# Loading and splitting the first pair of attention heads once for both heads

## Chip, cores and metric

One core of a Trainium2 chip runs the whole program. The metric is the device time of one execution in microseconds (us), lower is better. Three executions of the kernel before took 829.32, 829.61 and 830.26 us; the median is 829.61.

## The reference

Batch 2, 8 heads, sequence 1152, head size 64. Queries are averaged in pairs along the sequence, so each head has 576 query rows and 1152 keys. The attention output, laid out as 1152 tokens of 512 features, goes through a leaky-ReLU layer pair (512 to 2048 to 512) and then through four experts (512 to 1024 to 512), weighted by normalised probabilities.

```python
q_pool = q.reshape(B, H, S // 2, 2, D).mean(axis=3)
scores = (1 / sqrt(D)) * q_pool @ k.T
attn = softmax(scores)                    # row maximum taken off, 1e-9 in the denominator
x = (attn @ v)                            # to 1152 tokens x 512
x = leaky_relu(x @ w_in) @ w_out
out = sum_e p[:, e] * (relu(x @ w1[e]) @ w2[e])
```

All operands are float32. The kernel writes each operand of a product as a high part (cast to the multiplier's short float form) plus a low part (the rest), and adds up products of the parts.

## The kernel before

The eight (batch, pair of heads) units are called pairs, n = 0 to 7. A pair has nine tiles of 128 query rows: tiles 0 to 3 belong to the first head, tile 4 is half of each, tiles 5 to 8 belong to the second. Tile number i counts through all pairs, 72 in all. In this document S(i), T(i) and so on mean a step of tile i:

- S(i), `emit_s`: the score products on PE, in three chunks of 384 keys (L375). Then DVE copies the scores out of PSUM and takes their extreme, here called reduce(i) (L378).
- exp(i), `emit_exp`: the exponential on ACT (L384).
- sum(i) and norm(i), `emit_sum` and `emit_norm`: two tiny DVE steps (L388, L392) and then the scaling of the 128x1152 tile on POOL (L393).
- T(i), `emit_t`: nine transposes on PE (L414), three at a time; ACT casts each group to its high part (L418, `th`), and DVE takes the low part (L101, `tl`).
- AV, `queue_av` and `run_av`: the products of transposed scores with the values (L441), taken from a list a few at a time. When a chunk of the list is through, ACT and DVE add its two halves (L449, L450) and POOL splits the result (`xh`, `xl`).

The order on each engine's queue is the order in which the program issues instructions; it is written out by hand (`manual_schedule`), and an engine takes its queue strictly in that order. In the main loop, iteration i issues S(i+2) (in the first six tiles), sums and norms up to tile i+1, the steps in `early[i]`, T(i), some AV, exp(i+2) and then the steps in `steps[i]`.

For pairs 1 to 7 the keys and queries arrive once as 128 rows, 64 of each head (`rk_b`, `rq_b`), are split by `prep_pair` (POOL adds the two queries of each average, `q_add`, L306; ACT makes high parts; POOL makes low parts), and eight on-chip DMAs lay them out so that one product of 128 rows adds two terms: K of a head holds its high part in rows 0 to 63 and its low part in rows 64 to 127, and Q holds the same 64 rows twice. Two products per chunk then give all four terms. Tile 4 uses a block-diagonal operand `qmid` for its low terms.

Pair 0 is different. `first_pair` loads an input for each head that already holds the 64 rows twice (`q0`, `k0`, made on the host), so no on-chip copy is needed: `rk_b` and `rq_b` for head 0, `rk1` and `rq1` for head 1. SP issues these loads, then `load_v(0)`; ACT issues two pieces of keys. While they fly PE runs 18 transposes of no use (`keep_warm`). Head 0 is split in pieces, head 1 later in pieces between the first tiles (`k_hi(1, ..)`, `q_add(POOL, 1, ..)`, `q_hi(1, ..)`, `q_lo(POOL, 1, ..)` on L507 to L518 and in `steps`, `k_lo(DVE, 1, ..)` on L516 and L569). Because head 0 frees `rk_b` and `rq_b` early, `load_qk(1)` (L519), the keys and queries of pair 1, can start while head 1 is still being split.

The split of pair 1 begins in iteration 1: its `q_add` is in `early[1]`, on POOL's queue behind norm(2) and ahead of norm(3); its `k_hi` is in `steps[1]`.

Of the kernel before, what the change touches and what calls it, by code (L numbers as in the profile page):

```python
# [11 lines left out]
F32 = mybir.dt.float32  # L12
# [8 lines left out]
SQ = S // 2  # L21
# [12 lines left out]
def f32(ap):  # L34
    return ap.bitcast(F32)


@with_exitstack
def tile_kernel(ctx: ExitStack, tc: tile.TileContext, q, k, v, q0, k0, w_in, w_out, probs, w1, w2, out):
    nc = tc.nc  # L40
    PE, ACT, DVE, POOL, SP = nc.tensor, nc.scalar, nc.vector, nc.gpsimd, nc.sync

# [20 lines left out]
    rk1, rq1 = (at(f"r{i}1", 31872 + 2 * 2880 + 1152 * i, [S], F32) for i in range(2))  # L63
# [132 lines left out]
    with ExitStack() as actx:  # L196
# [17 lines left out]
        def two_heads(n, name):  # L214
            return [kv[name, h, n % 2] for h in range(2)]

        def load_qk(n):
            if n >= len(pairs):
                load_a()
                load_a()  # L220
                return
            b, p = pairs[n]
            rk, rq = rk_b, rq_b.rearrange("p (a b) -> p a b", a=2)
            SP.dma_start(rk, k[b, p])
            SP.dma_start(rq, q[b, p])
            raw[n] = (rk, rq)
# [8 lines left out]
        def first_pair():  # L235

            b, p = pairs[0]
            ks = kst[0] = two_heads(0, "k")
            rk = [rk_b, rk1]
            down = slice(64, 128)  # L240

            def halves(h, a, z):

                if h:
                    return rq1[:, a:z], rq1[:, SQ + a:SQ + z]
                o = next(x for x in (256, 128, 0) if a >= x)
                w = SQ - 256 if o == 256 else 128
                return rq_b[:, o + a:o + z], rq_b[:, o + w + a:o + w + z]
# [12 lines left out]
            load_v(0)

            def q_add(e, h, a, z):
                x, y = halves(h, a, z)
                e.tensor_tensor(x, x, y, op=ALU.add)

            def q_hi(h, a, z):
                hi(ACT, qst[0][:, 0, h, h * 64 + a:h * 64 + z], halves(h, a, z)[0])

            def q_lo(e, h, a, z):  # L270
                cs = slice(h * 64 + a, h * 64 + z)
                lo(e, qst[0][:, 1, h, cs], halves(h, a, z)[0], qst[0][:, 0, h, cs])

            def k_hi(h, a, z):
                hi(ACT, ks[h][:, a:z], rk[h][:, a:z])

            def k_lo(e, h, a, z):
                lo(e, ks[h][down, a:z], rk[h][down, a:z], ks[h][down, a:z])
            return q_add, q_hi, q_lo, k_hi, k_lo

        def prep_pair(n):


            rk, rq = raw.get(n, (None, None))

            rows = [slice(h * 64, h * 64 + 64) for h in range(2)]

            def k_hi():
                kh = k_hi_of[n] = kh_b[n % 2]
                hi(ACT, kh, rk)  # L290

# [12 lines left out]

            def q_add():
                POOL.tensor_tensor(rq[:, 0], rq[:, 0], rq[:, 1], op=ALU.add)  # L306

            def q_hi():
                hi(ACT, rq[:, 1].bitcast(F32R), rq[:, 0])

            def q_lo():
                lo(POOL, rq[:, 0].bitcast(F32R), rq[:, 0], rq[:, 1])
                t = qst[n % 2]
                for h in range(2):
                    r = slice(h * 64, h * 64 + 64)
                    hi(POOL, qmid[n % 2][r, r], rq[r, 0, (SQ - 64) * (1 - h):][:, :64])
                    for d in (slice(0, 64), slice(64, 128)):
                        SP.dma_start(f32(t[d, :, h, h * 64:h * 64 + SQ]), rq[r])

            def v_hi(h):  # L320
                if h == 0:
                    vst[n] = [t.rearrange("p (a b) -> p a b", a=NKB) for t in two_heads(n, "v")]
                a = h * 64
                hi(ACT, vst[n][h][:, :, a:a + 64], raw_v[n][:, :, h, :])

            def v_lo(h):
                a, c = h * 64, 64 - h * 64
# [30 lines left out]
        def emit_s(i):  # L358
            n, t = tiles[i]
            ps = three_banks(int(i == 1))  # L360
            Q, K = qst[n % 2], kst[n]
            if t < 4:
                use = [(0, t * 128)]
            elif t == 4:
# [2 lines left out]
                use = [(1, 128 + (t - 5) * 128)]  # L367
            for c in range(3):
                cs = slice(c * CW, (c + 1) * CW)
                mms = [(Q[:, j, h, c0:c0 + 128], K[h][:, cs]) for h, c0 in use for j in (1, 0)]  # L370
                if len(use) > 1 and n:

                    mms = mms[::2] + [(qmid[n % 2], k_hi_of[n][:, cs])]
# [93 lines left out]
                av.pop(0)[1]()  # L467

        with tc.manual_schedule():
            q_add, q_hi, q_lo, k_hi, k_lo = first_pair()  # L470

            DVE.memset(warm, 0.0)
            ACT.activation(warm, warm, AF.Exp)
# [27 lines left out]
            q_add(POOL, 0, 256, SQ)  # L501
# [46 lines left out]
            begin_at = {9 * m - P0: [m] for m in range(3, len(pairs))} | {P1: [0, 1], P2: [2]}  # L548
# [397 lines left out]
```

## Time and profile before

| | |
|---|---|
| median of three runs | 829.61 us |
| the profiled execution | 830.79 us |
| its span (first to last instruction) | 829.0 us |
| PE busy | 817.9 us |
| DVE, ACT, POOL busy | 567.7, 433.3, 407.2 us |
| mean granted TensorE clock | 0.998 of full |

The profiled execution took 830.79 us, 1.79 us more than its span, and 1.18 us more than the median of the runs. Busy time of PE is the sum of its instructions with modelled ends; a change is worth what it takes from or adds to the stretches in which PE waits or runs at a lower clock.

### The profile page before, as it was taken

To read this page: it belongs to the slowest core of one execution; us is meant where nothing else is said; L and a number is where in the kernel's file an instruction comes from. 1 tells how busy PE (TensorE), PEld (TensorE's weight loads), DVE (VectorE), ACT (ScalarE), POOL (GpSimd) and SP (SyncE) were. 2 spreads that over 40 slices of the span, in tenths; PEclk is the share of its full clock that TensorE was granted. 3 is DMA by queue.
4 is the path that set the end of the run, shared out by engine and by line. 5 is a ranking of instruction groups with operands and counts; after the bars stand their busy time and mean duration, and the time that the engine had idled before them with its cause. 6 is when DMAs were issued, how large, how long until landed. Compare 5 with 4: busy or idle time off the path is not lost.

```text
span 829.0 us, 13581 instructions
## 1 busy us (share of the span) xinstructions
PE 817.9 (99%) x5079; PEld 773.4 (93%) x5079; DVE 567.7 (68%) x955; ACT 433.3 (52%) x765; POOL 407.2 (49%) x363
## 2 busy tenths in 40 slices
PE   7899999999999999999999999999999999999998
PEld 6899999999999999999999989989898989989897
DVE  6899999999989898686766753627354453626332
ACT  7899999999985664334223632415051332505030
POOL 6798888888760487665550333306051332404020
PEclk9999999999999999999999999999999999999999
DMA  6626563664303333212220211203020111201012
GB/s 229 187 77 186 153 158 107 167 172 111 107 27 97 101 108 102 86 67 77 85 69 1 77 51 39 64 1 102 1 76 27 51 51 32 71 0 53 0 41 100
DMA packets 25969, 68.65 MB, mean 83 GB/s; under 512 B 2992, under 2 KB 7984, under 8 KB 25904
## 3 DMA queue, kind: packets, MB, share of 16 engines
q1 hardware_dynamic: 25616, 67.40, 27.6%
q8 instruction: 40, 0.66, 0.3%
q10 hardware_dynamic: 288, 0.39, 0.1%
q14 instruction: 25, 0.20, 0.1%
HBM read 48.91 MB, written 2.36 MB: 62 GB/s over the span
## 4 chain that ended last, share of the span: by engine, by line
PE 90%; DVE 6%; issue 1%; POOL 1%; DMA 1%; SPq 0%; ACT 0%; DVEq 0%; POOLq 0%; ACTq 0%
PE ps L762 22%; PE ps L375 8%; PE ps L807 8%; PE ps L809 8%; PE ps L808 8%; PE ps L441 8%; PE ps L414 7%; PE ps L191 4%; PE ps L190 4%; PE ps L659 4%; PE ps L660 4%; PE ps L192 4%; PE ps L661 4%; DVE e L378 2%; DVE tl L101 2%
## 5 line engine op out<-in xcount | busy, mean ns | idle before, releaser
L101 POOL TENSOR_TENSOR bb<-w2r,bb 128x512 fp32r<-128x512 f32 x32 | 40.8, 1296 | 258.9 <-ACT bb L94 258.9
L816 DVE SCALAR_TENSOR_TENSOR oacc<-ps,pw,oacc 128x512 f32<-128x512 f32 (+1 forms) x64 | 47.5, 742 | 100.4 <-PE ps L809 100.4
L101 DVE TENSOR_TENSOR tl<-ps,th 128x384 fp32r<-128x384 f32 (+1 forms) x240 | 111.9, 505 | 3.6 <-ACT th L418 2.8
L807 PE MATMUL ps<-bb,gg 128*128 128x512 f32 (+1 forms) x292 | 112.9, 387 | 0.0
L809 PE MATMUL ps<-bb,gg 128*128 128x512 f32 (+1 forms) x292 | 112.9, 386 | 0.0
L808 PE MATMUL ps<-bb,gg 128*128 128x512 f32 (+1 forms) x292 | 112.8, 386 | 0.0
L762 PE MATMUL ps<-yT,ws 128*128 128x288 f32 x768 | 111.5, 296 | 0.0
L762 PEld LDWEIGHTS ps<-yT,ws 128*128 128x128 f32 x768 | 105.7, 189 | 0.9 <-ACT cb L779 0.3
L393 POOL TENSOR_SCALAR e<-e,st 128x1152 f32<-128x1152 f32 x72 | 89.2, 1239 | 33.0 <-DVE st L392 18.3
L378 DVE TENSOR_SCALAR_CACHE_REDUCE e<-ps 128x1152 f32<-128x1152 f32 x72 | 97.4, 1354 | 9.0 <-PE ps L375 7.8
L418 ACT CAST th<-ps 128x384 fp32r<-128x384 f32 (+1 forms) x240 | 91.3, 459 | 13.6 <-PE ps L414 11.7
L768 ACT COPY ca<-ps 128x576 f32<-128x576 f32 x16 | 10.2, 639 | 167.1 <-PE ps L762 155.3
L375 PE MATMUL ps<-k,qst 128*128 128x384 f32 x438 | 94.4, 345 | 3.2 <-DVE e L378 1.6
L384 ACT ACTIVATE e<-e,st 128x1152 f32<-128x1152 f32 x72 | 91.3, 1268 | 2.5 <-DVE e L378 0.8
L414 PE MATMUL ps<-ident,e 128*128 128x128 f32 x648 | 83.8, 275 | 2.9 <-POOL e L393 2.2
L762 PE MATMUL ps<-yB,ws 128*128 128x288 f32 x576 | 84.4, 296 | 0.0
L375 PEld LDWEIGHTS ps<-k,qst 128*128 128x128 f32 x438 | 75.5, 190 | 8.1 <-DVE e L378 4.4
L414 PEld LDWEIGHTS ps<-ident,e 128*128 128x128 f32 x648 | 75.1, 141 | 7.5 <-POOL e L393 4.2
L762 PEld LDWEIGHTS ps<-yB,ws 128*128 128x128 f32 x576 | 79.8, 189 | 0.6
L809 PEld LDWEIGHTS ps<-bb,gg 128*128 128x128 f32 x292 | 54.8, 188 | 11.4 <-DVE gg L788 0.2
L101 DVE TENSOR_TENSOR ws<-wf,ws 128x768 fp32r<-128x768 f32 (+1 forms) x32 | 44.3, 1386 | 30.1 <-ACT ws L94 30.1
L808 PEld LDWEIGHTS ps<-bb,gg 128*128 128x128 f32 x292 | 54.8, 188 | 10.6
(130 smaller groups left out, 1730.5 us busy)
## 6 DMA issues: line engine op xcount, KB each, us to landing
wa<-in_w_in SPq DMA_DIRECT2D x16, 512.0 KB, 3.6
wb<-in_w_out SPq DMA_DIRECT2D x16, 512.0 KB, 4.5
wf<-in_w SPq DMA_DIRECT2D x32, 256.0 KB, 2.8
w2r<-in_w SPq DMA_DIRECT2D x16, 512.0 KB, 3.6
qst<-rq SPq DMA_DIRECT2D x28, 288.0 KB, 4.8
rv<-in_v SPq DMA_DIRECT2D x8, 576.0 KB, 5.8
rk<-in_k SPq DMA_DIRECT2D x7, 576.0 KB, 5.9
rq<-in_q SPq DMA_DIRECT2D x7, 576.0 KB, 4.8
```

The costliest lines, as they stand in the source:

```text
L101: eng.tensor_tensor(dst, src, f32(high), op=ALU.subtract)
L375: PE.matmul(ps[:, c, :CW], x, y, start=m == 0, stop=m == len(mms) - 1)
L378: DVE.tensor_scalar(e, ps[:, :, :CW], -0.5 / float(D) ** 0.5, None, op0=ALU.mult, op1=ALU.min, accum_out=st[:, 0:1])
L384: ACT.activation(e, e, AF.Exp, bias=st[:, 0:1], scale=-1.0, accum_out=st[:, 1:2])
L393: POOL.tensor_scalar(e, e, st[:, 3:4], 1.0, op0=ALU.mult, op1=ALU.mult)
L414: PE.transpose(ps[:, j], e[:, (3 * g + j) * 128:(3 * g + j + 1) * 128], ident)
L418: ACT.copy(h, ps[:, :, s0:s0 + w])
L441: PE.matmul(cell["ps"][:, :w], V, part[:, kb, :w], start=m == 0, stop=last)
L762: PE.matmul(ps[:, c, :HW], w[wi][:, i, ks], y[:, yi, k, c * HW:(c + 1) * HW], start=bool(first and k == 0 and m == 0), stop=k == 1 and m = ...
L807: PE.matmul(ps, gh[:, ts_], wh, start=f == fs[0], stop=False)
L808: PE.matmul(ps, gh[:, ts_], wl, start=False, stop=False)
L809: PE.matmul(ps, gl[:, ts_], wh, start=False, stop=f == fs[-1])
```

## The change

Pair 0 is loaded like the others: 128 rows, 64 of each head, once. The host still reorders the queries of pair 0 into three runs of columns, and the keys come straight from the common input. The split of keys is done on all 128 rows at once: `kh_b[0]` takes the high part, a new tile `kl0` the low part.

Tiles 0 to 4 then use three products of 128 rows per chunk: low Q by high K, high Q by high K, high Q by low K. Q has zeros in the rows of the other head: for tiles 0 to 3 a new POOL memset puts them into `qst[0][64:, :, 0]`; tile 4 uses both `qmid` tiles, filled by `q_mid`. Tiles 0 to 3 had two products per chunk and now have three; tile 4 had four and now has three.

For tiles 5 to 8 the old layout of head 1 is made by DMAs on the chip: `k_out` (two, 288 KB each) and `q_out` (one, 288 KB). `k_out` and `load_k(1)` are issued right after the split of the keys. `load_q(1)` and `load_v(1)` come behind `q_out` on SP's queue.

The second head's own work is left out in part: no `q_add`, `k_hi` and `k_lo` for head 1. Its `q_hi` is three ACT instructions, its `q_lo` three POOL instructions, all on 64 rows. `q_mid` adds four POOL instructions of 64x64. Ten transposes of no use between the first tiles instead of six (`keep_warm(2)` twice, new).

```diff
-            SP.dma_start(rk[1], k0[1])
-            SP.dma_start(rq1, q0[1])
             load_v(0)
...
+            def k_out():
+                ks = kst[0] = two_heads(0, "k")
+                for d, t in ((up, kh), (down, kl0)):
+                    SP.dma_start(f32(ks[1][d]), f32(t[down]))
+
+            def q_mid(h):
+                r = (up, down)[h]
+                for j in range(2):
+                    hi(POOL, qmid[j][r, r], f32(qs[r, j, h, (SQ - 64) * (1 - h) + 64 * h:][:, :64]))
+
+            def q_out():
+                SP.dma_start(f32(qs[up, :, 1, 64:64 + SQ]), f32(qs[down, :, 1, 64:64 + SQ]))
+
+            def products(t, cs):
+                x = qmid if t == 4 else [qs[:, j, 0, t * 128:t * 128 + 128] for j in range(2)]
+                return [(x[1], kh[:, cs]), (x[0], kh[:, cs]), (x[0], kl0[:, cs])]
...
-                k_hi(0, c * CW, (c + 1) * CW)
-                k_lo(DVE, 0, c * CW, (c + 1) * CW)
+                k_hi(c * CW, (c + 1) * CW)
+                k_lo(DVE, c * CW, (c + 1) * CW)
+            k_out()
+            load_k(1)
...
             upto("s", emit_s, 0)
+            keep_warm(2)
             q_lo(POOL, 0, 128, 256)
             upto("s", emit_s, 1)
...
+            q_mid(0)
             upto("exp", emit_exp, 0)
             upto("sum", emit_sum, 0)
             upto("norm", emit_norm, 0)
-            k_hi(1, 0, CW)
+            keep_warm(2)
             upto("s", emit_s, 2)
             upto("exp", emit_exp, 1)
             keep_warm(6)
-            k_hi(1, CW, 2 * CW)
-            q_add(POOL, 1, 0, 192)
-            q_hi(1, 0, 192)
+            q_hi(1, 0, SQ)
             upto("sum", emit_sum, 1)
             upto("norm", emit_norm, 1)
-            k_lo(DVE, 1, 0, CW)
-            q_lo(POOL, 1, 0, 192)
-            q_add(POOL, 1, 192, SQ)
-            load_qk(1)
+            q_lo(POOL, 1, 0, 128)
+            q_mid(1)
+            q_lo(POOL, 1, 128, 256)
+            q_lo(POOL, 1, 256, SQ)
+            q_out()
+            load_q(1)
             load_v(1)
...
-            steps = {0: [lambda: k_hi(1, 2 * CW, S)],
-                     1: [lambda: q_hi(1, 192, SQ), lambda: q_lo(POOL, 1, 192, SQ)]}
+            steps = {0: [lambda: v_hi(0)], 1: [lambda: v_lo(0)], 4: [lambda: v_hi(1)], 5: [lambda: v_lo(1)]}
...
-                if i < 2:
-                    k_lo(DVE, 1, (i + 1) * CW, (i + 2) * CW)
```

## Rows read from the trace of the kernel before

**Rows 1.** Busy time by stretch: start:end us, length, busy us (count), clock, DMA share, GB/s.
```profile
15.00:20.00 5.00, 4.38 (x29) 3.83 (x30) 4.87 (x14) 5.00 (x11) 3.62 (x4) 1.00 0.02 8
40.65:829.00 788.35, 784.30 (x4885) 743.49 (x4883) 536.62 (x881) 402.17 (x703) 379.29 (x326) 1.00 0.26 77
```

**Rows 2.** The chain of waits, 0 to 45 us: start us, length us, what.
```profile
9.90 1.33 PE ps L375 x6
...
12.92 1.03 DVE k L101 x2
...
17.88 1.24 POOL e L393
...
21.01 1.02 POOL qst L101
...
23.30 1.20 PE ps L414 x9
```

**Rows 3.** POOL in order of time: start, length, line, operation, [idle before <-releaser].
```profile
5.69 0.46 POOL L265 TENSOR_TENSOR rq<-rq 128x128 f32<-128x128 f32 x1 [3.56 <-DMA rq<-in_q]
...
13.06 1.91 POOL L393 TENSOR_SCALAR e<-e,st 128x1152 f32<-128x1152 f32 x1 [0.21 <-DVE st L392]
...
19.08 1.97 POOL L306 TENSOR_TENSOR rq<-rq 128x576 f32<-128x576 f32 x1
...
23.20 1.43 POOL L101 TENSOR_TENSOR rk<-rk,kh 128x576 fp32r<-128x576 f32 x1
...
29.16 1.22 POOL L393 TENSOR_SCALAR e<-e,st 128x1152 f32<-128x1152 f32 x1
```

**Rows 4.** POOL, groups by line and shape, 0 to 100 us: count | busy us, mean ns.
```profile
L306 POOL TENSOR_TENSOR rq<-rq 128x576 f32<-128x576 f32 x3 | 4.8, 1603 | 0.0
...
L96 POOL TENSOR_SCALAR qmid<-rq 64x64 fp32r<-64x64 f32 x6 | 1.4, 239 | 0.5
...
L101 POOL TENSOR_TENSOR qst<-rq,qst 128x320 fp32r<-128x320 f32 x1 | 0.9, 862 | 0.6 <-ACT qst L94 0.6
...
L205 POOL MEMSET qst<- 128x128 f32 x2 | 0.4, 204 | 0.0
```

**Rows 5.** PE in order of time, matmuls only.
```profile
16.80 2.36 PE L375 MATMUL ps<-k,qst 128*128 128x384 f32 x12 [0.56 <-DVE e L378]
...
21.52 1.21 PE L375 MATMUL ps<-k,qst 128*128 128x384 f32 x6
...
27.93 1.34 PE L375 MATMUL ps<-k,qst 128*128 128x384 f32 x6 [0.57 <-DVE e L378]
30.43 1.93 PE L414 MATMUL ps<-ident,e 128*128 128x128 f32 x9 [1.17 <-POOL e L393]
32.02 1.68 PE L441 MATMUL ps<-th,v 128*128 128x320 f32 x5
33.50 1.50 PE L375 MATMUL ps<-k,qst 128*128 128x384 f32 x6
34.84 1.15 PE L414 MATMUL ps<-ident,e 128*128 128x128 f32 x9
35.74 0.83 PE L441 MATMUL ps<-th,v 128*128 128x320 f32 x4
```

**Rows 6.** DMAs: SP's issue, then issues of `qst` (ns min/median/max).
```profile
9.88 0.33 SPq L225 DMA_DIRECT2D rq<-in_q  x1
...
L318 SPq DMA_DIRECT2D qst<-rq x4: 608/741/1482, 27.3 to 29.5; - x4
```

**Rows 7.** Issue to landing, us: loads at 36.28 and 67.98; four `qst` copies.
```profile
rk<-in_k SPq DMA_DIRECT2D x1, 576.0 KB, 3.8
...
rq<-in_q SPq DMA_DIRECT2D x1, 576.0 KB, 4.4
...
DMA to landing us min/median/max: 3.3/5.2/6.0
```

**Rows 8.** A stretch after the fall of the clock, columns as in Rows 1.
```profile
31.00:31.50 0.50, 0.50 (x4) 0.50 (x3) 0.23 (x3) 0.33 (x1) 0.50 (x1) 0.50 0.93 171
```

More of the change, by code (lines that the diff above doesn't have):

```diff
@@ L38, in tile_kernel @@
 @with_exitstack
-def tile_kernel(ctx: ExitStack, tc: tile.TileContext, q, k, v, q0, k0, w_in, w_out, probs, w1, w2, out):
+def tile_kernel(ctx: ExitStack, tc: tile.TileContext, q, k, v, q0, w_in, w_out, probs, w1, w2, out):
     nc = tc.nc
@@ L61, in tile_kernel @@
     rk_b, rq_b = (at(n, 46976 + 1152 * i, [S], F32) for i, n in enumerate(("rk", "rq")))
-    rk1, rq1 = (at(f"r{i}1", 31872 + 2 * 2880 + 1152 * i, [S], F32) for i in range(2))
+    kl0 = at("kl0", 31872 + 2 * 2880, [S])
     rv_b = [at(f"rv{i}", o, [S], F32) for i, o in enumerate((49280, 51264))]
@@ L203, in tile_kernel @@
         make_identity(nc, ident)
+        POOL.memset(f32(qst[0][64:, :, 0]), 0.0)
         for t in qst:
@@ L215, in two_heads, with load_k, load_q @@
             return [kv[name, h, n % 2] for h in range(2)]
+        def load_k(n):
+            SP.dma_start(rk_b, k[pairs[n]])
+        def load_q(n):
+            raw[n] = (rk_b, rq_b.rearrange("p (a b) -> p a b", a=2))
+            SP.dma_start(raw[n][1], q[pairs[n]])
         def load_qk(n):
@@ L221, in load_qk @@
                 return
[L222 to L226, printed above, removed]
+            load_k(n)
+            load_q(n)
         def load_v(n):
@@ L237, in first_pair @@
             b, p = pairs[0]
[L238 to L248, printed above, removed]
+            rk, kh, qs = rk_b, kh_b[0], qst[0]
+            up, down = slice(0, 64), slice(64, 128)
             def key_part(c):
-                return rk[0][:, c * CW:(c + 1) * CW], k0[0][:, c * CW:(c + 1) * CW]
-            SP.dma_start(rq_b[:, :256], q0[0][:, :256])
+                cs = slice(c * CW, (c + 1) * CW)
+                return rk[:, cs], k[b, p][:, cs]
+            SP.dma_start(rq_b[:, :256], q0[:, :256])
             ACT.dma_start(*key_part(0))
@@ L256, in first_pair, with runs @@
             SP.dma_start(*key_part(2))
-            SP.dma_start(rq_b[:, 256:512], q0[0][:, 256:512])
-            SP.dma_start(rq_b[:, 512:], q0[0][:, 512:])
-            SP.dma_start(rk[1], k0[1])
-            SP.dma_start(rq1, q0[1])
+            SP.dma_start(rq_b[:, 256:512], q0[:, 256:512])
+            SP.dma_start(rq_b[:, 512:], q0[:, 512:])
             load_v(0)
-            def q_add(e, h, a, z):
-                x, y = halves(h, a, z)
-                e.tensor_tensor(x, x, y, op=ALU.add)
+            def runs(rows, a, z):
+                even, odd, x = [], [], a
+                while x < z:
+                    o = next(y for y in (256, 128, 0) if x >= y)
+                    w = SQ - 256 if o == 256 else 128
+                    y = min(z, o + w)
+                    even.append((x, y, rq_b[rows, o + x:o + y]))
+                    odd.append(rq_b[rows, o + w + x:o + w + y])
+                    x = y
+                return even, odd
@@ L267, in q_hi, with q_add @@
+            def q_add(e, a, z):
+                for (_, _, x), y in zip(*runs(slice(0, 128), a, z)):
+                    e.tensor_tensor(x, x, y, op=ALU.add)
             def q_hi(h, a, z):
-                hi(ACT, qst[0][:, 0, h, h * 64 + a:h * 64 + z], halves(h, a, z)[0])
+                r = (up, down)[h]
+                for x, y, src in runs(r, a, z)[0]:
+                    hi(ACT, qs[r, 0, h, h * 64 + x:h * 64 + y], src)
             def q_lo(e, h, a, z):
-                cs = slice(h * 64 + a, h * 64 + z)
@@ L272, in q_lo @@
[L272 to L279, printed above, removed]
+                r = (up, down)[h]
+                for x, y, src in runs(r, a, z)[0]:
+                    cs = slice(h * 64 + x, h * 64 + y)
+                    lo(e, qs[r, 1, h, cs], src, qs[r, 0, h, cs])
@@ new lines, in k_hi, with k_lo @@
+            def k_hi(a, z):
+                hi(ACT, kh[:, a:z], rk[:, a:z])
+            def k_lo(e, a, z):
+                lo(e, kl0[:, a:z], rk[:, a:z], kh[:, a:z])
+            def k_out():
[3 more added lines that the diff above has]
+            def q_mid(h):
+                r = (up, down)[h]
+                for j in range(2):
+                    hi(POOL, qmid[j][r, r], f32(qs[r, j, h, (SQ - 64) * (1 - h) + 64 * h:][:, :64]))
@@ L281, in prep_pair @@
+            def q_out():
[3 more added lines that the diff above has]
+                return [(x[1], kh[:, cs]), (x[0], kh[:, cs]), (x[0], kl0[:, cs])]
+            return q_add, q_hi, q_lo, k_hi, k_lo, k_out, q_mid, q_out, products
         def prep_pair(n):
@@ L330, in prep_pair @@
             if n == 0:
-                return [[lambda: v_hi(0)], [lambda: v_lo(0)], [], [], [lambda: v_hi(1)], [lambda: v_lo(1)]]
+                return v_hi, v_lo
             qk = [[q_add, k_hi], [k_all], [q_hi], [q_lo, lambda: load_qk(n + 1)]]
@@ L360, in emit_s @@
             ps = three_banks(int(i == 1))
-            Q, K = qst[n % 2], kst[n]
+            Q, K = qst[n % 2], kst.get(n)
             if t < 4:
@@ L369, in emit_s @@
                 cs = slice(c * CW, (c + 1) * CW)
-                mms = [(Q[:, j, h, c0:c0 + 128], K[h][:, cs]) for h, c0 in use for j in (1, 0)]
+                if i < 5:
+                    mms = products(t, cs)
+                else:
+                    mms = [(Q[:, j, h, c0:c0 + 128], K[h][:, cs]) for h, c0 in use for j in (1, 0)]
                 if len(use) > 1 and n:
@@ L469, in tile_kernel @@
         with tc.manual_schedule():
-            q_add, q_hi, q_lo, k_hi, k_lo = first_pair()
+            q_add, q_hi, q_lo, k_hi, k_lo, k_out, q_mid, q_out, products = first_pair()
             DVE.memset(warm, 0.0)
@@ L480, in tile_kernel @@
             keep_warm(18)
-            q_add(DVE, 0, 0, 128)
+            q_add(DVE, 0, 128)
             q_hi(0, 0, 128)
@@ L484, in tile_kernel @@
             for c in range(3):
-                k_hi(0, c * CW, (c + 1) * CW)
-                k_lo(DVE, 0, c * CW, (c + 1) * CW)
+                k_hi(c * CW, (c + 1) * CW)
+                k_lo(DVE, c * CW, (c + 1) * CW)
+            k_out()
+            load_k(1)
+            v_hi, v_lo = prep_pair(0)
             at = dict.fromkeys(("s", "exp", "sum", "norm"), 0)
@@ L493, in upto @@
                     at[what] += 1
-            q_add(POOL, 0, 128, 256)
+            q_add(POOL, 128, 256)
             q_hi(0, 128, 256)
             upto("s", emit_s, 0)
+            keep_warm(2)
             q_lo(POOL, 0, 128, 256)
             upto("s", emit_s, 1)
-            q_add(POOL, 0, 256, SQ)
+            q_add(POOL, 256, SQ)
             q_hi(0, 256, SQ)
             q_lo(POOL, 0, 256, SQ)
+            q_mid(0)
             upto("exp", emit_exp, 0)
@@ L545, in tile_kernel @@
                 ahead.setdefault(t, []).append(load)
-            begin_at = {9 * m - P0: [m] for m in range(3, len(pairs))} | {P1: [0, 1], P2: [2]}
-            steps = {0: [lambda: k_hi(1, 2 * CW, S)],
-                     1: [lambda: q_hi(1, 192, SQ), lambda: q_lo(POOL, 1, 192, SQ)]}
+            begin_at = {9 * m - P0: [m] for m in range(3, len(pairs))} | {P1: [1], P2: [2]}
+            steps = {0: [lambda: v_hi(0)], 1: [lambda: v_lo(0)], 4: [lambda: v_hi(1)], 5: [lambda: v_lo(1)]}
             for i, (n, t) in enumerate(tiles):
```

10 lines of the change are left out of this document (2 added, 8 removed).

## The prediction

> **What bounds the kernel now.** I read the busy time by stretch first. From 40.65 us to the end PE is busy for 784.30 of 788.35 us [rows 1]; there every instruction waits for PE, and the change does not touch that part. Whatever the change is worth is decided before, while PE still waits for pair 0 to be split. In 15 to 20 us ACT is busy for 5.00 of 5.00, DVE for 4.87, PE for 4.38 and the DMA engines hardly at all (share 0.02) [rows 1]. So the opening is a relay between engines, not a lack of bandwidth.
>
> Then the chain of waits: S(2) at 9.90, DVE's `k_lo` for head 1 at 12.92, norm(2) at 17.88, head 1's `q_lo` at 21.01, and T(3) at 23.30 [rows 2]. From 16 us on the chain runs over POOL: norm(2), `q_add` of pair 1 (19.08), `q_lo` of head 1 (21.01), norm(3), and T(3) as soon as norm(3) is through. After T(3) POOL keeps the lead: eight instructions without a gap to speak of, from 23.20 to the end of norm(5) at 29.16 + 1.22 = 30.38 [rows 3], and T(5) starts at 30.43 [rows 5]. After that PE is nearly full. So I ask one thing: when does norm(3) end, and with it T(3)? A shift there is passed on by POOL to T(5), and by PE to the end.
>
> **The change part by part.**
>
> *The first tiles.* The loads that gate S(0) to S(2) have the same sizes as before. The two loads that shared the wires with them are gone, but POOL's work up to S(2) is in-order and keeps the same number of elements, so I leave S(2) at 9.90 and put a gain of up to 0.5 us into the range. The new memset (64 rows, 1280 elements) is bounded by 0.20 us, the price of a 128x128 one [rows 4], and ten times that for ten times the elements, 2.04. I take the upper end; POOL then sits idle 3.56 us for the first queries [rows 3], which hides it. The four new useless transposes stand where PE waits for POOL or DVE anyway; I cost them at nothing, and at 4 x 0.13 (1.15 us for nine, [rows 5]) if that wait is gone.
>
> *Products.* Twelve take 2.36 us and six take 1.21 us [rows 5], so one more takes (2.36 - 1.21) / 6 = 0.19. Tiles 0 to 3 get three more each, 0.57; tile 4 gets three fewer. Net nine, 1.7 us of PE time. S(0), S(1) and S(3) lie beside key splits, reductions and norms. S(2) does not: reduce(2), sum(1) and norm(1) follow it directly. So norm(1) starts at 13.06 + 0.57 = 13.63.
>
> *What leaves DVE, ACT and POOL.* Head 1's `k_lo` (three of 0.52, from 1.03 for two [rows 2]) leaves DVE, so sum(2) and norm(2) come 0.5 earlier: 17.88 becomes 17.35 and ends at 18.6. Norm(1) took 1.91 us while two of these `k_lo` ran on DVE, against 1.22 for norm(5) [rows 3]. Without them I take 1.24, so norm(1) ends at 14.87, 0.1 earlier than before. ACT loses three casts and splits `q_hi` in three; T(1) and its casts stay where they were. On POOL head 1's `q_add` goes, 1.6 us.
>
> *The moved step.* Pair 1's `load_q` was issued at 9.88 [rows 6], because head 1 had its own buffer. Now head 1's queries lie in `rq_b` until POOL's last `q_lo`, and `load_q(1)` stands on SP's queue behind `q_out`, which waits for the same `q_lo`. Behind norm(1) POOL does `q_lo` of 128, `q_mid` (two of 0.24), `q_lo` of 128 and of 320 (0.86) [rows 4]. For 128 columns I take 0.46, the price of `q_add` of that size [rows 3]: 0.46 + 0.48 + 0.46 + 0.86 = 2.26, so POOL is done at 17.13. Then SP issues `q_out`: 0.61 to 1.48, median 0.74 [rows 6]. `load_q(1)` starts at 17.9. It lands 3.8 us after issue if it is like the load at 36.28, which was the first of its group, or 4.4 like the one at 67.98 [rows 7]. The DMA engines were idle at this time [rows 1], so I take 3.8: 21.7. `load_v(1)`, behind it on SP, is used late and costs nothing.
>
> *The new wait.* POOL reaches `q_add` of pair 1 at 18.6 and waits until 21.7, 3.1 us. Behind it on POOL's queue stands norm(3), and T(3) waits for that. `q_add` cost 1.97 in its one place here, with DVE's `v_lo` beside it; the group of three makes the other two (4.8 - 1.97) / 2 = 1.42 [rows 3, 4]. In the new order `v_lo` is over by 19.3, so I take 1.43. Then norm(3), 1.24 with its handover 1.3: 21.7 + 1.43 + 1.3 = 24.45. T(3) goes from 23.30 to about 24.47, later by 1.17. PE has nothing else: S(5) ends near 22.2 (21.52 + 1.21, less the 0.5 that DVE gained) [rows 5], so PE idles for 2.3 us where it idled 0.6.
>
> A page sets another price for the load: the Trainium skill, "DMA: Bandwidth & Descriptors", section "Anatomy of one DMA — SWDGE (gpsimd) path", gives 2.0 us plus bytes over 436 GB/s, which is an estimate of 3.35 us for these 590 KB and would make the shift 0.7 instead of 1.17. No row of this case is below 3.8 for that size, so the row stands.
>
> *The sum.* T(3) +1.17, passed on by POOL's eight instructions to T(5), then by PE. The profiled execution took 830.79 us with a span of 829.0; with the shift it would take 831.96. It lies 1.18 above the median of the runs, so against that median the forecast is 829.61 + 1.17 = 830.8.
>
> Bounds of this case: `q_lo` done 0.7 earlier (S(2) 0.5 earlier, the short issue) gives 830.1; a landing of 4.4 and `q_add` at 1.97 give +0.6 and +0.5, 831.9.
>
> **Rivals.**
>
> *The clock moves with the stall.* After waits of 0.57 and 1.17 us around S(7), the granted clock was 0.50 in 31.0 to 31.5, the 1.2 GHz level [rows 5, 8]. T(5) then took 1.93 instead of 1.15, the five AV products 1.68 instead of 5/4 x 0.83 = 1.04, S(8) 1.50 instead of 1.21 [rows 5]: 1.7 us in all. If the new idle of 2.3 us makes the clock fall before T(3), the slow products fill PE's spare time before T(5), the later fall has no cause, and 1.7 comes back: 830.8 - 1.7 = 829.1. For it: the new gap is longer than both old ones together. Against it: a fall may come at both places, and the clock before 30 us rests on one execution.
> The Trainium skill, "TensorE: Matmul & The Clock Gate", section "HAM oscillation — how this bites in real kernels", says that a burst of products behind each long wait starts slow. By that rule a slow T(3) is to be expected; no row here shows what follows.
>
> *The load is in time, or its wait is covered.* If POOL's `q_lo` ends early and POOL's saved 1.6 us counts in full, `q_add` follows norm(2) at 18.6, norm(3) ends at 21.3, and T(3) comes right behind S(5) at 22.2, 1.1 earlier: 828.5. If the clock then doesn't fall at T(5), another 1.7: 826.8. For it: work really leaves three full engines. Against it: the load would have to be issued before 14.8, when norm(1) has not ended.
>
> *The load queues behind `q_out`.* Place: SP's queue. Both are issued 0.7 us apart, and of four 288 KB copies issued in a row the first took 3.3 us and the last 6.0 [rows 7], 0.9 more for each copy ahead. With that price the load lands at 22.6, T(3) is later by 2.07, and the time is 831.7. This case decides for slower from a landing of 4.3 us on. For it: the later load at 67.98 took 4.4. Against it: only one copy is ahead, and the four wrote more scattered rows than one load.
>
> **How the numbers follow.** The forecast has a chance of 0.45, the moved clock 0.2, the load in time 0.15, the queue 0.2. About 0.2% (1.66 us, so 827.95 and 831.27) is what a measurement can tell from no change. Of the forecast's 0.45 a third lies above 831.27 by its bounds (0.15); the queue lies above with 0.17 of 0.2. Slower: 0.32. Faster needs the load in time together with the clock (0.1) or a clock gain with the short bounds of the forecast (0.06): 0.16. The rest is no change: 0.52. The range goes from 828.1, which takes in the moved clock and most of the load in time, to 832.2, the queue with the forecast's upper bounds. The likeliest case's own range is 830.1 to 831.9.
>
> **What would show it.** Right: `load_q(1)` issued near 17.9; a wait of about 3 us of POOL for `rq` ahead of the 576-column `q_add`; T(3) near 24.5; norm(1) near 1.24 us. Wrong: POOL with no wait for a DMA after 15 us, T(3) before 23.3, or PE idle before T(3) under 1 us. The clock rival would show a granted clock of 0.50 soon after T(3) and 1.00 at T(5).

## The result, and the profile after

| | before | after |
|---|---|---|
| median of four runs of each | 829.54 us | 835.08 us |
| lowest to highest | 829.32 to 830.26 | 833.0 to 835.34 |
| ratio, 95% interval | | 1.006, 1.0042 to 1.0077 |
| profiled execution | 830.79 us | 835.07 us |
| PE busy | 817.9 us | 820.0 us |

The change costs 5.5 us. The forecast was 830.8, and the time lies above the range. Line numbers below are those of each kernel; in the changed one L406 is the score products, L424 norm, L445 the transposes, L334 `q_add`, L302 `q_out`, L204 the new memset.

Busy time by stretch, kernel after (start:end, length, busy us of PE, PEld, DVE, ACT, POOL with counts, clock, DMA share, GB/s):

```profile
15.00:20.00 5.00, 4.43 (x30) 4.08 (x28) 4.56 (x11) 4.97 (x10) 4.22 (x7) 1.00 0.12 27
20.00:25.00 5.00, 3.58 (x28) 3.24 (x26) 4.75 (x11) 3.65 (x8) 0.42 (x1) 1.00 1.01 307
25.50:27.00 1.50, 0.00 (x0) 0.00 (x0) 0.00 (x0) 0.67 (x1) 1.50 (x2) 0.50 0.78 163
30.00:31.00 1.00, 1.00 (x6) 1.00 (x5) 0.53 (x1) 0.05 (x1) 1.00 (x1) 0.50 0.97 224
40.65:829.00 788.35, 787.21 (x4903) 746.38 (x4902) 539.28 (x889) 405.41 (x707) 381.84 (x327) 1.00 0.26 78
```

Against [rows 1] the long last stretch is as full as it was (787.21 of 788.35), so again everything is decided before it. In 20 to 25 us POOL works 0.42 of 5 us while the DMA engines are full. From 25.5 us on the granted clock is 0.50, the 1.2 GHz level; it is back at 1.00 from 32.5.

The chain of waits, kernel after, from the start (start us, us, what):

```profile
1.01 1.16 POOL qst L204
2.24 0.30 POOL ident masks.py:199
2.59 4.10 PE ps L511 x18
6.69 2.43 PE ps L406 x9
...
18.73 1.24 POOL e L424
19.97 4.57 issue
24.58 0.11 POOL rq L334
24.78 1.17 issue
25.96 1.24 POOL e L424
27.24 2.18 PE ps L445 x9
```

The new memset stands at the head of the chain. "Issue" of 4.57 us behind norm(2) is POOL's wait; the 1.17 us of it at 24.78 lie within `q_add`. POOL in order of time says for whom ([idle before <-releaser]):

```profile
0.99 1.16 POOL L204 MEMSET qst<- 64x1280 f32 x1
...
14.59 1.24 POOL L424 TENSOR_SCALAR e<-e,st 128x1152 f32<-128x1152 f32 x1 [0.58 <-ACT qst L94]
...
16.77 1.29 POOL L101 TENSOR_TENSOR qst<-rq,qst 64x128 fp32r<-64x128 f32 x2
18.73 1.24 POOL L424 TENSOR_SCALAR e<-e,st 128x1152 f32<-128x1152 f32 x1 [0.67 <-ACT th L449]
24.58 1.40 POOL L334 TENSOR_TENSOR rq<-rq 128x576 f32<-128x576 f32 x1 [4.61 <-DMA rq<-in_q]
```

The last two `q_lo` end at 16.77 + 1.29 = 18.06. SP's issues follow it, and then the landings of the same DMAs (count, KB, us from issue to landing):

```profile
18.09 0.65 SPq L302 DMA_DIRECT2D qst<-qst  x1
18.83 0.55 SPq L223 DMA_DIRECT2D rq<-in_q  x1
```

```profile
rq<-in_q SPq DMA_DIRECT2D x1, 576.0 KB, 5.7
...
qst<-qst SPq DMA_DIRECT2D x1, 288.0 KB, 3.2
```

PE, matmuls in order of time, kernel after, to be held against [rows 5]:

```profile
22.37 1.21 PE L406 MATMUL ps<-k,qst 128*128 128x384 f32 x6
27.24 2.18 PE L445 MATMUL ps<-ident,e 128*128 128x128 f32 x9 [3.66 <-POOL e L424]
29.07 1.84 PE L472 MATMUL ps<-tl,v 128*128 128x256 f32 x7
30.71 1.95 PE L406 MATMUL ps<-k,qst 128*128 128x384 f32 x6
...
35.89 1.20 PE L445 MATMUL ps<-ident,e 128*128 128x128 f32 x9 [0.34 <-POOL e L424]
```

S(5) ends near 23.6 (22.2 in the forecast), then PE stands for 3.66 us. T(3) comes at 27.24 instead of 23.30 and takes 2.18 instead of 1.20; S(6) takes 1.95 instead of 1.21. T(5) is at 35.89 instead of 30.43, later by 5.46, which is the loss. So the loss has two parts: 3.94 us up to T(3), and 1.52 us between T(3) and T(5) (8.65 us against 7.13).

The second part ends in a new wait of POOL. DVE and POOL in order of time, kernel after: the reduction and the last step of the sum, then the norm:

```profile
32.80 1.36 DVE L409 TENSOR_SCALAR_CACHE_REDUCE e<-ps 128x1152 f32<-128x1152 f32 x1 [1.02 <-PE ps L406]
...
34.26 0.16 DVE L423 RECIPROCAL st<-st 128x1 f32<-128x1 f32 x1
```

```profile
34.60 1.24 POOL L424 TENSOR_SCALAR e<-e,st 128x1152 f32<-128x1152 f32 x1 [1.53 <-ACT th L449]
```

These are reduce(6), sum(5) and norm(5). S(6) ends late on the slow PE, reduce(6) waits for it, sum(5) stands behind reduce(6) on DVE's queue, and norm(5) starts 0.18 us after sum(5). (The view names a cast of T(4), which norm(5) does not read.) In before POOL went from norm(3) to norm(5) without such a wait.

That T(5) carries the whole time holds for the experiments too. Profiled executions, all in us:

| kernel | T(0) | T(3) | T(5) | T(3) to T(5) | time | time less T(5) |
|---|---|---|---|---|---|---|
| before | 12.35 | 23.30 | 30.43 | 7.13 | 830.79 | 800.36 |
| after | 14.06 | 27.24 | 35.89 | 8.65 | 835.07 | 799.18 |
| e1 memset on DVE | 12.86 | 25.77 | 32.90 | 7.13 | 832.17 | 799.27 |
| e2 own buffer | 13.12 | 22.48 | 29.33 | 6.85 | 828.83 | 799.50 |
| e3 both | 12.82 | 22.18 | 29.04 | 6.86 | 828.38 | 799.34 |
| e4 values late | 13.65 | 28.65 | 36.26 | 7.61 | 835.40 | 799.14 |
| e6 `q_add` behind norm(3) | 13.12 | 22.46 | 32.02 | 9.56 | 831.23 | 799.21 |
| e7 gap filled | 14.09 | 27.08 | 34.22 | 7.14 | 833.58 | 799.36 |
| e10 two products | 11.88 | 22.18 | 28.77 | 6.59 | 828.15 | 799.38 |

Behind T(5) all take 799.1 to 799.5. Only the profiled execution of before has 1.2 more: its clock fell at T(5) [rows 5, 8], which is also the 1.18 by which it lies above its median. With 799.2 for the rest, before's T(5) at 30.43 gives 829.6, its median. The 61 runs of before that stand beside the experiments fit: the 9 with a mean granted clock of 0.998 have a median of 830.26, the 41 at 1.000 one of 829.44.

### The profile page after: what moved, and what is told of

It reads as the page before. It is cut to its first block, busy times and chain, and to the rows that moved or that the text cites. A ratio compares the mean times of both kernels' runs of the same rounds, so it can differ in the third digit from the quotient of the medians.

```text
span 833.3 us, 13608 instructions
## 1 busy us (share of the span) xinstructions
PE 820.0 (98%) x5092; PEld 777.0 (93%) x5092; DVE 566.1 (68%) x952; ACT 432.6 (52%) x763; POOL 407.2 (49%) x367
## 3 DMA queue, kind: packets, MB, share of 16 engines
q1 hardware_dynamic: 25632, 67.11, 27.3%
## 4 chain that ended last, share of the span: by engine, by line
PE 91%; DVE 6%; issue 2%; POOL 1%; ACT 0%; DVEq 0%; POOLq 0%; ACTq 0%
PE ps L796 21%; PE ps L406 8%; PE ps L843 8%; PE ps L841 8%; PE ps L842 8%; PE ps L472 8%; PE ps L445 7%; PE ps L693 4%; PE ps L191 4%; PE ps L190 4%; PE ps L694 4%; PE ps L192 4%; PE ps L695 4%; DVE e L409 2%; DVE tl L101 1%
## 5 line engine op out<-in xcount | busy, mean ns | idle before, releaser
L424 POOL TENSOR_SCALAR e<-e,st 128x1152 f32<-128x1152 f32 x72 | 88.8, 1234 | 34.8 <-DVE st L423 17.7
L445 PE MATMUL ps<-ident,e 128*128 128x128 f32 x648 | 84.0, 275 | 5.2 <-POOL e L424 5.0
L406 PE MATMUL ps<-k,qst 128*128 128x384 f32 x402 | 86.6, 345 | 1.3 <-DVE e L409 0.9
L445 PEld LDWEIGHTS ps<-ident,e 128*128 128x128 f32 x648 | 75.3, 142 | 9.6 <-POOL e L424 6.2
L406 PEld LDWEIGHTS ps<-k,qst 128*128 128x128 f32 x402 | 69.7, 190 | 4.6 <-DVE e L409 3.6
```

The lines of the kernel that those rows point to most:

```text
L406: PE.matmul(ps[:, c, :CW], x, y, start=m == 0, stop=m == len(mms) - 1)
L424: POOL.tensor_scalar(e, e, st[:, 3:4], 1.0, op0=ALU.mult, op1=ALU.mult)
L445: PE.transpose(ps[:, j], e[:, (3 * g + j) * 128:(3 * g + j + 1) * 128], ident)
```

## The experiments

Medians stand against the kernel before on the same chip in the same rounds (829.46 to 829.61). Each diff is against the changed kernel unless it says otherwise.

**e1: the memset on DVE.**

```diff
-        POOL.memset(f32(qst[0][64:, :, 0]), 0.0)
...
+            DVE.memset(f32(qst[0][64:, :, 0]), 0.0)
             DVE.memset(warm, 0.0)
```

> The new memset of 64x1280 goes from POOL, where it ran 1.16 us ahead of the last step of the identity, to DVE, which is idle there. Theory (two separate losses: the memset holds back PE's warm-up, and the load of pair 1's queries holds back POOL): the 18 transposes start at 1.5 instead of 2.6, T(0) comes 1.1 to 1.7 us earlier than 14.06, POOL's last q_lo ends 1.1 to 1.5 earlier than 18.06, the load as much earlier, T(3) near 25.9 instead of 27.24, and the clock still falls: time 1 to 2 us under the changed kernel's 835.1. Rival (the load alone decides): T(3) stays within 0.3 of 27.24 and the time within 0.5.

Measured: 832.17 (831.99 to 833.35, five runs), ratio 1.0034 (1.0021 to 1.0048), 2.9 less than after. PE and POOL in order of time, kernel e1:

```profile
12.86 1.20 PE L444 MATMUL ps<-ident,e 128*128 128x128 f32 x9 [0.66 <-POOL e L423]
...
25.77 1.20 PE L444 MATMUL ps<-ident,e 128*128 128x128 f32 x9 [3.39 <-POOL e L423]
```

T(0) is 1.20 earlier and T(3) 1.47. The other 1.52 us come between T(3) and T(5): PE waited nearly as long as in after, 3.39 us, but the granted clock stayed at 1.00 and T(3) took 1.20. In the profiled execution the gain is larger than was expected because the fall of the clock went as well, which was not in either expectation. The other four runs have mean clocks of 0.995 to 0.998, and three of them took 831.99 to 832.34 all the same: where the clock fell in them is not on record, and a lower mean clock does not by itself cost time.

**e2: the first pair's queries in a buffer of their own.** `load_q(1)` then waits for nothing and stands right behind `load_k(1)`.

```diff
+    rq0 = at("rq0", 31872 + 2 * 2880 + 1152, [S], F32)
...
-            SP.dma_start(rq_b[:, :256], q0[:, :256])
+            SP.dma_start(rq0[:, :256], q0[:, :256])
...
             load_k(1)
+            load_q(1)
...
             q_out()
-            load_q(1)
             load_v(1)
```

> Pair 0's queries get a buffer of their own (the place that the changed kernel leaves free), so the load of pair 1's queries is issued right behind its keys near 7.7 us and no longer behind q_out; the memset stays on POOL. Theory: POOL's wait of 4.61 us goes, its 576-column q_add follows norm(2) at about 20, T(3) follows S(5) near 23.6 instead of 27.24, and the clock does not fall before T(3): time 3.6 to 5.5 us under 835.1, between 829.6 and 831.5. Rival (the products, DMAs and extra steps of the change cost as much): time over 832.

Measured: 828.85 (828.33 to 829.53, ten runs), 0.999 (0.9981 to 1.0), 6.2 less than after. T(3) is at 22.48, right behind S(5); behind its first wait for queries POOL waits for no DMA. So the shared buffer, with the late load that it forces, is the cause of the loss, the clock's part included: without the stall T(3) takes 1.14 and T(5) follows after 6.85 us. The time lies under the 829.6 that was the least expected, as S(5) ends 0.94 earlier than in after; e6, with no edit in the opening, has nearly the same lead (0.96).

**e3: e1 and e2 together.** The diff is the two above.

> Both edits: memset on DVE and a buffer of its own for pair 0's queries with the early load. Theory: the two losses add up, so T(0) near 12.5 to 12.9, T(3) near 22.2 to 22.5, time 5 to 7 us under 835.1, that is 828 to 830, at or under the kernel before. Rival (nine more products and four more POOL steps cost by themselves): 1 us or more over the kernel before.

Measured: 828.17 (827.64 to 828.68, ten runs), 0.9985 (0.9975 to 0.9994): 1.36 us faster than before, 6.9 than after, the version that beats both. POOL and PE in order of time, kernel e3:

```profile
18.67 1.95 POOL L334 TENSOR_TENSOR rq<-rq 128x576 f32<-128x576 f32 x1
...
22.18 1.14 PE L445 MATMUL ps<-ident,e 128*128 128x128 f32 x9
...
29.04 1.21 PE L445 MATMUL ps<-ident,e 128*128 128x128 f32 x9 [0.59 <-POOL e L424]
```

T(5) moves 1.39 against before. The memset brings only 0.7 on top of e2, against 2.9 on top of after: where T(3) no longer carries a stall, there is no fall to avoid. That is 1.5 of the 2.2 us between the two; the rest fits the faster opening of e2 (T(0) at 13.12, against 14.06 in after).

**e4: pair 1's values loaded later**, so that less moves beside `load_q(1)`.

```diff
             load_q(1)
-            load_v(1)
...
-            steps = {0: [lambda: v_hi(0)], 1: [lambda: v_lo(0)], 4: [lambda: v_hi(1)], 5: [lambda: v_lo(1)]}
+            steps = {0: [lambda: v_hi(0)], 1: [lambda: v_lo(0)], 2: [lambda: load_v(1)], 4: [lambda: v_hi(1)], 5: [lambda: v_lo(1)]}
```

> Only the load of pair 1's values is moved: from right behind the load of its queries to the end of iteration 2. Theory (the query load took 5.7 us because q_out and the values, 288 and 576 KB, were in flight beside it): it lands in 3.8 to 4.6 us, POOL's wait falls from 4.6 to 3 to 3.7, T(3) is 1 to 1.8 earlier, time 0.9 to 1.8 under 835.1 with the clock's fall kept, more if the fall goes. Rival (it queues behind q_out or waits for something else): landing stays over 5.2 and the time within 0.5.

Measured: 835.04 (834.54 to 837.92, four runs), 1.0074 (1.0056 to 1.0092): nothing gained. Landing and POOL, kernel e4:

```profile
rq<-in_q SPq DMA_DIRECT2D x1, 576.0 KB, 7.5
```

```profile
25.99 1.40 POOL L334 TENSOR_TENSOR rq<-rq 128x576 f32<-128x576 f32 x1 [6.44 <-DMA rq<-in_q]
```

The landing got worse, which neither theory had. With the values gone, the next on SP's queue behind the load are two on-chip copies of pair 1's keys, issued at 20.88, while the load was in flight (18.37 to 25.87). That they are the cause was not tried by itself; e11 below has neither behind it and lands at 5.5.

**e5 and e11: the load by itself.** Both put pair 1's values into `steps[3]` and its key copies behind the split of its queries, so that nothing follows the load closely. e11 keeps `q_out` ahead of it; e5 leaves `q_out` out too and fills its rows with zeros on DVE. Diff of e5 (e11 has neither the memset nor the removed `q_out`):

```diff
-                qk = [[], [k_hi, lambda: k_out(0)],
-                      [q_hi, lambda: k_lo(0, SQ), lambda: k_out(1, 0, SQ)], [],
+                qk = [[], [k_hi],
+                      [q_hi, lambda: k_lo(0, SQ), lambda: k_out(1, 0, SQ), lambda: k_out(0)], [],
...
+            DVE.memset(f32(qst[0][:64, :, 1, 64:64 + SQ]), 0.0)
             DVE.memset(warm, 0.0)
...
-            q_out()
             load_q(1)
-            load_v(1)
...
+            steps = {0: [lambda: v_hi(0)], 1: [lambda: v_lo(0)], 3: [lambda: load_v(1)], 4: [lambda: v_hi(1)], 5: [lambda: v_lo(1)]}
```

> The load of pair 1's queries runs with no other DMA beside it: q_out is left out (its target rows are zeroed instead, so the second head of pair 0 is not computed), and the next two copies and the load of pair 1's values are put behind copies that wait for the load. Theory (the load is slow because the on-chip copies and the values share the engines with it): it lands 3.6 to 4.2 us after its issue instead of 5.7, POOL's wait is 2.6 to 3.3 us, and T(3) comes 1.2 to 1.7 us nearer to the end of norm(2) than the 8.5 us of the changed kernel (18.73 to 27.24). Rival (the load is slow by itself in this place): landing over 5.

> The changed kernel with q_out kept ahead of the load of pair 1's queries, but nothing behind it: the values of pair 1 and the next copies come behind copies that wait for the load. Theory (each DMA beside it takes its share): landing between the 3.8 of the load alone and 5.7, near 4.6; POOL's wait about 3.4. Rival (q_out alone is what slows it): landing over 5.2. Other rival (only what is issued behind it slows it): landing 4.0 or less.

Measured: 836.15 (834.83 to 837.46, two runs; 1.0077, 1.0054 to 1.0099) and 838.48 (one run). Both lose later, where S(9) waits for the delayed key copies, so only the stretch up to T(3) is read. Landings, kernel e5, then kernel e11:

```profile
rq<-in_q SPq DMA_DIRECT2D x1, 576.0 KB, 3.8
```

```profile
rq<-in_q SPq DMA_DIRECT2D x1, 576.0 KB, 5.5
qst<-qst SPq DMA_DIRECT2D x1, 288.0 KB, 3.3
```

POOL and PE, kernel e5:

```profile
21.74 1.44 POOL L334 TENSOR_TENSOR rq<-rq 128x576 f32<-128x576 f32 x1 [2.01 <-DMA rq<-in_q]
...
24.43 1.20 PE L445 MATMUL ps<-ident,e 128*128 128x128 f32 x9 [1.08 <-POOL e L424]
```

Alone the load lands in the 3.8 us of the forecast; T(3) is then at 24.43, against 24.47 forecast. That agreement of T(3) is in part luck: `q_lo` ended at 17.80, 0.67 after the forecast's 17.13, and the 0.74 for `q_out`'s issue is not in e5. POOL's wait, 2.01, is shorter than was expected for want of that issue. One copy of 288 KB issued 0.74 us ahead makes it 5.5. So 1.7 of the 1.9 us come from `q_out`, as e11's rival had it; the values behind the load add 0.2 at most (5.4 in e1 and 5.5 in e6 and e7 with them, 5.7 in after).

**e6: `q_add` of pair 1 behind norm(3)**, which leaves the load as it is and takes norm(3) from behind the wait.

```diff
-                early.setdefault(1, []).append(q_add)
+                early.setdefault(2, []).append(q_add)
```

> Only the place of pair 1's first q_add on POOL is changed: behind norm(3) instead of ahead of it. Theory (the load's wait costs because norm(3) stands behind it on POOL's queue): norm(3) ends near 21.2, T(3) follows S(5) near 23.5 instead of 27.24, and the wait now holds back norm(4) by less, so the time is 2 to 5 us under 835.1. Rival (the load itself, not the queue, sets the pace: everything of pair 1 waits for it): time within 1 us of 835.1.

Measured: 832.04 (831.23 to 832.88, seven runs), 1.0029 (1.0017 to 1.004), 3.0 less than after. T(3) is at 22.46, right behind S(5). But `q_add`'s wait moved on: T(4) waits 1.73 for `tl`, T(5) 1.58 for POOL, and T(5) is at 32.02. The order on POOL's queue is what turns the late load into a late T(3); another order alone gives back half of the loss.

**e7: 16 transposes of no use in PE's gap before T(3).**

```diff
+                if i == 3:
+                    keep_warm(16)
                 emit_t(i, norms)
```

> Sixteen transposes of no use ahead of T(3), in the gap of 3.66 us in which PE waits; nothing else. Theory (the fall of the clock in the gap costs about 2 us of the 5.5): T(3) starts where it started, the granted clock stays at 1.00 after it, T(3) takes 1.2 instead of 2.18, and the time is 1 to 2.2 us under 835.1. Rival (the slow products are hidden behind POOL up to T(5)): time within 0.5 us although the clock stays up.

Measured: 833.52 (833.41 to 833.76, four runs), 1.0046 (1.0031 to 1.0061), 1.56 less than after. PE in order of time, kernel e7:

```profile
23.44 1.91 PE L511 MATMUL ps<-ident 128*128 128x128 f32 x16
27.08 1.20 PE L445 MATMUL ps<-ident,e 128*128 128x128 f32 x9 [1.73 <-POOL e L424]
```

T(3) starts at the same time (27.08 against 27.24), takes 1.20, and T(5) follows after 7.14 us instead of 8.65. That is the price of the fall in after, 1.5 us in the trace and 1.56 in the medians: PE is slow behind the stall, not within it, so the two add up. DVE and POOL, kernel e7, to be held against the same three steps in after:

```profile
30.30 1.36 DVE L409 TENSOR_SCALAR_CACHE_REDUCE e<-ps 128x1152 f32<-128x1152 f32 x1 [0.31 <-PE ps L406]
...
31.77 0.16 DVE L423 RECIPROCAL st<-st 128x1 f32<-128x1 f32 x1
```

```profile
32.94 1.22 POOL L424 TENSOR_SCALAR e<-e,st 128x1152 f32<-128x1152 f32 x1
```

Here sum(5) is through at 31.93; with the 0.18 us from sum to norm, norm(5) has 0.83 us to spare, since POOL's queue brings it at 32.94. In after reduce(6) starts 5.56 us behind T(3), here 3.22: 2.34 more, less the 0.83, is the 1.5. The price depends on how long the clock stays down. In e4 and e11 it fell too, reduce(6) starts 4.51 and 4.79 behind T(3), and the same sum gives 0.46 and 0.74; T(3) to T(5) is 0.48 and 0.75 over 7.13.

**e8: the kernel before, with a POOL memset of 64x1152 at the same place.**

```diff
         make_identity(nc, ident)
+        POOL.memset(f32(kh_b[0][64:, :]), 0.0)
```

> The kernel before, with one POOL memset of 64x1152 (on a tile that nothing uses yet) at the place of the new one. Theory (the memset delays the identity and with it PE's warm-up by 1.1 us): the transposes start at 2.5 instead of 1.46, S(0) at 6.3 to 6.5 instead of 5.43, time 0.5 to 1.7 us over the kernel before. Rival (POOL is idle there, so it is hidden): time within 0.3.

Measured: 830.37 (829.76 to 830.97, ten runs), 1.0008 (0.9999 to 1.0017), 0.76 more than before at the medians, with an interval that just holds no change. In its trace the identity's last step comes at 2.14 instead of 1.11 and the 18 transposes at 2.48 instead of 1.46, yet T(0) only 0.10 later than before, and T(3) and T(5) 0.11 earlier (23.19 and 30.32). So the delay of the start is shown, and its way to the end is not. Among runs with a mean clock of 1.000 the difference is 0.5 (829.99, five runs, against 829.48, eleven).

**e9: e3 without the two new `keep_warm(2)`.**

```diff
             upto("s", emit_s, 0)
-            keep_warm(2)
...
             upto("norm", emit_norm, 0)
-            keep_warm(2)
```

> The kernel of e3 without the four useless transposes between S(0), S(1) and S(2) (two calls of keep_warm(2)). Theory (they stand on the path, since S(1) follows S(0) without a wait for POOL): T(0) 0.2 to 0.5 earlier than 12.82, time 0 to 0.5 us under e3's 828.2. Rival (they keep the clock up): the clock falls in the opening and the time is over 829.

Measured: 828.22 (827.82 to 832.2, ten runs), 0.9988 (0.9977 to 0.9999): the same as e3. The four transposes cost nothing, as forecast. In its profiled execution T(0) is 0.91 earlier, and the lead is lost again at S(5), kernel e9:

```profile
22.62 1.31 PE L406 MATMUL ps<-k,qst 128*128 128x384 f32 x6 [2.14 <-DMA qst<-qst]
```

S(5) waits there for `q_out`, which took 5.8 us to land instead of 3.2 in e3; why stays open. That execution took 829.28, a us above its median, so this wait need not be in most of them.

**e10: e3 with two products per chunk in tiles 0 to 3**, low Q by high K left out there.

```diff
-                return [(x[1], kh[:, cs]), (x[0], kh[:, cs]), (x[0], kl0[:, cs])]
+                return [(x[1], kh[:, cs])][:t == 4] + [(x[0], kh[:, cs]), (x[0], kl0[:, cs])]
```

> The kernel of e3 with two products per chunk in tiles 0 to 3: the low part of Q by the high part of K is left out there, so these scores are less exact. Twelve products of 384 columns are gone. Theory (S(0), S(1) and S(3) are on the path now, at 0.18 to 0.26 us a product): time 0.8 to 2 us under e3's 828.2. Rival (as I costed them, only S(2) counts and the rest is hidden): 0 to 0.6 under.

Measured: 828.01 (827.68 to 829.6, ten runs), 0.9982 (0.9972 to 0.9991), 0.16 under e3. Twelve products fewer, 2.3 us of PE at 0.19 each, are worth nothing that can be told. T(0) is 0.94 earlier, T(3) at 22.18 as in e3. DVE and POOL in order of time, kernel e10:

```profile
17.41 1.42 POOL L334 TENSOR_TENSOR rq<-rq 128x576 f32<-128x576 f32 x1
17.46 1.99 DVE L102 TENSOR_TENSOR v<-rv,v 128x576 fp32r<-128x576 f32 x1
```

With the lead POOL starts `q_add` just ahead of DVE's `v_lo`, which then takes 1.99 us; PE's first AV products wait 0.80 for it, norm(3) 1.05 for ACT's casts.

**e12: e3 with `q_add` of pair 1 ahead of norm(2).**

```diff
-                early.setdefault(1, []).append(q_add)
+                early.setdefault(0, []).append(q_add)
```

> The kernel of e3 with pair 1's q_add ahead of norm(2) on POOL, where it no longer runs beside DVE's v_lo. The load lands at 14.4 there, so nothing waits for it. Theory (POOL's queue is what T(5) waits for, 0.59 us in e3): q_add takes 1.43 instead of 1.95, norm(2) is 0.8 later, norm(3) to norm(5) 0.5 earlier, time 0.2 to 0.6 under e3. Rival (norm(2) is on the path): time 0.3 to 0.8 over e3.

Measured: 828.73 (828.32 to 829.33, ten runs), 0.9991 (0.9981 to 1.0), 0.56 over e3. `q_add` gets its 1.44 us, but norm(2) stands behind it: T(2) waits 1.51 for POOL, so the rival was right. With its data there in time, `q_add` is better placed between norm(2) and norm(3).

## Why the prediction was wrong

The mechanism was right: `load_q(1)` became late because the queries share `rq_b`, POOL waited for it ahead of `q_add`, norm(3) stood behind that wait, and T(3) set the end (e2 and e6 show it). Right in size were norm(1) (1.24), `q_add` (1.40 for 1.43), the copy's issue (0.74 from one issue to the next), the four transposes (e9) and that the end follows T(5).

The step that failed first is the moved step: "The DMA engines were idle at this time [rows 1], so I take 3.8". They were idle in before; in the new order `q_out` was in them, issued 0.74 us earlier by the same plan. The landing was 5.7, and T(3) was 1.9 later for it. Without `q_out` it is 3.8 (e5). This is the third rival's mechanism; that rival was given 0.2 and priced at 0.9 for a copy ahead, from four copies among themselves [rows 7]. The price is 1.7 (e11), twice that.

The second is the opening, and the memset in it: "POOL then sits idle 3.56 us for the first queries [rows 3], which hides it". POOL's idle time lies behind the memsets, but this one ran between the two steps of the identity, although the source has it behind `make_identity`, and PE's first transposes wait for the second step. PE started at 2.59 instead of 1.46, S(2) came at 10.91 instead of 9.90, and POOL's `q_lo` ended at 18.06 against the forecast 17.13, 0.93 late; on DVE (e1) it ends at 16.86.

The 0.93 is not the memset's alone. PE in order of time, kernel after, then kernel e6, whose program is the same up to here and whose transposes also start at 2.59: the first two products of S(0), and the two transposes behind S(0):

```profile
6.34 0.99 PE L406 MATMUL ps<-kh,qst 128*128 128x384 f32 x2
...
8.96 0.38 PE L511 MATMUL ps<-ident 128*128 128x128 f32 x2
```

```profile
6.35 0.63 PE L406 MATMUL ps<-kh,qst 128*128 128x384 f32 x2
...
8.03 0.38 PE L511 MATMUL ps<-ident 128*128 128x128 f32 x2
```

S(0) is 0.94 longer in after. In e6 `q_lo` ends at 17.10, as forecast, with the memset where it was; in the seven profiled executions with the memset in this place and `keep_warm` unchanged (after, e2, e4 to e7, e11) it ends between 16.59 and 18.06, and T(0) lies between 12.61 and 14.09. On DVE T(0) is 12.82 and 12.86. At the medians the memset is worth 0.76 (e8, where the interval just holds no change) and 0.68 (e3 against e2); the rest of the 0.93 goes with the slow first products, whose cause stays open.

With 0.93 and 1.9 the sum's T(3) goes from 24.47 to 27.3; measured 27.24.

The third is the clock, which the sum put at nothing although it had PE idle 2.3 us before T(3). The first rival had the fall before T(3), and the later one gone, as happened (T(5) took 1.20). But it said that 1.7 "comes back". The forecast counted from the median, and most runs of before hold no such fall (830.79 against a median of 829.54), so nothing was there to come back; and the early fall costs 1.5 (e7). PE's spare time between T(3) and T(5) is there, as the rival had it, but it is 0.83 us and the slow products took 2.34; POOL's eight instructions no longer lead to T(5), as norm(5) waits 1.53 for a sum behind S(6). The run of after that took 833.0 had a mean clock of 1.000, the other three 0.996.

So 1.17 forecast, 1.9 for the late landing (1.7 of it the copy ahead), 0.93 for the late opening and 1.5 for the clock make 5.5. The useful part of the change, which the second rival described (828.5), is real: e3 has it, at 828.17, with the load issued at 7.96 and the memset on DVE, and e2 at 828.85 with the early load alone.

The three products were put on the path with 0.57 up to norm(1); e10 takes them away and T(3) does not move. Nothing of them is seen at the end.

## What to carry to other kernels

Where a change saves a load by sharing a buffer, ask first who used that buffer next, and which work stands in queue behind the one that now waits. Price a transfer with what the new order itself puts ahead of it on the wires, not by the idle share of the old trace. An engine's idle time hides added work only if nothing that others wait for is queued behind that work; look at the first instruction, not at the largest gap.

## What the runs showed of the hardware

While the copy of 64 rows inside the chip ran, the DMA engines were full and moved half of what they moved for the load of 128 rows behind it. Busy time by stretch, kernel e11, columns as before (`q_out` issued at 16.61, `load_q(1)` at 17.35):

```profile
18.00:19.00 1.00, 1.00 (x9) 0.87 (x8) 1.00 (x2) 1.00 (x3) 0.51 (x1) 1.00 1.01 221
19.00:20.00 1.00, 1.00 (x11) 1.00 (x10) 0.97 (x4) 1.00 (x2) 0.00 (x0) 1.00 0.98 212
20.00:21.00 1.00, 1.00 (x11) 1.00 (x10) 1.00 (x3) 1.00 (x4) 0.00 (x0) 1.00 0.98 392
```

The engines' share is full throughout; while the copy runs they move 212 to 221 GB/s, and 392 after it. The Trainium skill, "SBUF — State Buffer", section "Door 1: The DMA port swizzle (why `[64,N]` ≈ `[32,N]`)", says that 64 partitions reach 8 of 16 ports and gives about 218 GB/s as their limit; this trace agrees. No run here tells the number of rows from the copy's being inside the chip as the reason.

Where DVE's `v_lo` and POOL's `q_add` met, the one that began later stretched. In e3 `v_lo` begins first (18.57, 0.75 us) and `q_add` takes 1.95; in e10 `q_add` begins first (17.41, 1.42) and `v_lo` takes 1.99. Each time the later one ends 1.30 or 0.62 us behind the end of the first, a little less than it takes alone (1.42 and 0.75), as if it had stood still. The same page, the Trainium skill's "SBUF — State Buffer", section "Who interferes with whom", says that the issue order decides which one blocks; these two rows agree.

Seven executions of the same opening put T(0) anywhere from 12.61 to 14.09. In after the first two products with high K took 0.99 us and the next two 0.84, in e6 0.63 and 0.51, with the granted clock column at 1.00 in both. What makes PE slow there stays open. So does what lets the clock fall with a wait of 3.66 us in after and of 3.43 in e11 and not with one of 3.39 in e1.
